# A gated recurrent attention with two MLPs on one core: elementwise steps between VectorE and GpSimd, longer filler pieces, a new order of all steps

## The chip, the core and the metric

The kernel runs on one core of a Trainium2 chip. Of that core's engines it uses TensorE (PE, matrix products), VectorE (DVE), ScalarE (ACT), GpSimd (POOL), and SyncE (SP), whose queue issues all DMAs. The metric is the device time of one execution in microseconds; the lower the better.

## The reference, cut to what matters

A recurrence over 768 steps for 2 x 8 heads of 40, its output as 1536 tokens of 320, then two MLPs over these tokens. All data is float32.

```python
def _attn_ref(q, k, v, i_gate, f_gate, o_gate):      # (2, 8, 768, 40), gates (2, 8, 768)
    for t in range(S):
        m_new = np.maximum(f_gate[:, :, t] + m, i_gate[:, :, t])
        f_stab = np.exp(f_gate[:, :, t] + m - m_new)
        i_stab = np.exp(i_gate[:, :, t] - m_new)
        m = m_new
        C = f_stab[...] * C + i_stab[...] * np.einsum('bhd,bhe->bhde', vt, kt)
        n = f_stab[...] * n + i_stab[...] * kt
        h_tilde = np.einsum('bhde,bhe->bhd', C, qt)
        denom = np.maximum(np.abs(np.einsum('bhd,bhd->bh', n, qt)[:, :, None]), 1.0)
        y[:, :, t] = sigmoid(o_gate[:, :, t]) * h_tilde / denom

def _moe_ref(x, w_a, w_b, w_out):                    # 1536x320, 320x1536 twice, 1536x320
    return (x @ w_a) * (x @ w_b) @ w_out

def _moe2_ref(x, w_in, w_out):                       # 320x2048, 2048x320
    h = x @ w_in
    return (h * sigmoid(h)) @ w_out
```

## The kernel before

The 1536 tokens are twelve tiles of 128 (`u0` to `u11`; even tiles belong to the first batch entry, odd ones to the second). The recurrence is worked out a tile at a time: products of queries and keys (`s0`, "scores"), weighed on DVE with running products of the forget gates (`w0 w1`), times the values (`v0 v1`); what the tile adds to the state (`upd`) and what the state gives to the tile (`car`). Around them stand small steps: scaled keys and values (`sk sv si`), the state carried on (`am`, or `ao ae`, `bo be`), the output's parts put together (`cb0 cb1 cc`), its denominator (`da dn rc`), the gate (`sig om`), the tile of 320 outputs (`ox xt`), its transposes on PE (`px`) and the split of these into a high and a low part (`xh xl`).

The gates of all steps come first, on DVE and ACT: a scan (`run0` for the first 128 steps, `run1` for the other 640), sums and differences (`pl mi ii`), exponentials (`expf expi`), a second scan (`pr`), columns by transposes on PE (`pg0`, copied out by DVE), and the decay factors of the first four tiles by products on PE (`u0.f0` to `u3.f0`) that DVE scans (`d0`).

Float32 products run as float32r products of split operands: every operand is kept as a high part and the rest. For the weights of the first MLP (twelve tiles `w0` to `w11` of 128 hidden columns) this is `p s0 s1 o0 o1` (put together from the loaded words), `h t` (high parts), `u la lb` (the rest; `u` goes by two small DMAs `v0 v1`). For the second MLP's sixteen tiles it is `p s o h ho l t lo` of `x0` to `x15`. `lw` and `lx` load them; `l0.k`, `l0.t`, `l2.e` load queries and keys, the `kvo` tile and stored gate factors.

An MLP pass holds some token tiles and walks over hidden tiles: `m0` two token tiles and hidden tiles 0 to 4, `m1` the next two, `m2` these four with hidden tiles 5 to 11, `m3` and `m4` four tiles each with all twelve; `n0 n1 n2` are the second MLP, four token tiles and sixteen hidden tiles each. For a hidden tile, `a` and `b` are eight PE products each into a PSUM bank (the "h" products; the second MLP has `b` alone), `e` moves a's out, `g` multiplies with b's (for the second MLP `g` is the activation), `h` takes the high part, `l` the rest, `c` is the second layer: three products of 320 columns for each token tile, added up in "acc" banks. `z0` to `z3` evict a pass's token tiles and, in the second MLP, store them.

All of it stands in one hand-written list, ORDER. The program walks over it and issues each step's instructions; an engine runs its own instructions in that order, and waits on semaphores for others. A suffix sets the engine of a step that has a choice: `:v` is DVE, `:p` POOL. Without a suffix, a copy goes to ACT and a two-operand step (`both`, `rest`) to POOL. Eight PSUM banks go round; the hidden tiles have two buffers for each of `g` (by `e` or `g`) and `g2` (by `h` and `l`), two raw buffers take the first MLP's loaded weights.

Thirty steps `f0` to `f29` are fillers: products of a bfloat16 identity with itself into a bank that nobody reads. All of them are placed ahead of the first MLP's products.

Of the kernel before, what the change touches and what calls it, by code (L numbers as in the profile page):

```python
# [68 lines left out]
m3.7.g m3.11.c m4.1.a m3.7.h m3.7.l y1.px y1.xh y1.xl m3.9.h m3.9.l m4.1.b x0.lo lx2 x2.p x2.s x2.o x2.h x2.ho x2.t
m3.7.c m3.9.c m3.z1 m3.z3 m3.z0 y5.xt m4.7.a m4.7.e lx3 x3.p x3.s x3.o x3.ho m3.z2 x2.l x3.lo m4.7.b m4.7.g m4.7.h  # L70
x3.h y2.px y2.xh y2.xl m4.7.l x3.l m4.3.a m4.3.e m4.3.b m4.3.g m4.3.h m4.3.l x2.lo x3.t m4.1.e:v m4.1.g lx5 y3.px
m4.0.a m4.0.e y3.xh m4.0.b m4.0.g m4.10.a m4.3.c m4.10.b m4.7.c m4.2.a m4.1.h:p m4.1.l m4.1.c x5.p x5.s x5.o x5.h
x5.ho x5.l x5.t m4.10.e:v m4.10.g m4.10.h m4.10.l m4.10.c lx10 y3.xl x10.p x10.s x10.o m4.0.h m4.0.l x5.lo m4.2.e
x10.h x10.l x10.t x10.ho x10.lo lx9 x9.p x9.s x9.o x9.h x9.ho x9.lo m4.2.b m4.2.g m4.5.a m4.5.e:v m4.5.b m4.5.g
y0.px y0.xh y0.xl m4.0.c m4.8.b lx4 x4.p m4.11.b m4.11.a x9.l x9.t m4.4.a m4.5.h m4.5.l m4.5.c m4.11.e m4.11.g
m4.11.h m4.11.l m4.4.b lx8 x8.p x8.s x8.o x8.h x8.t x8.ho x8.lo x4.s x4.o x4.ho x8.l x4.lo m4.2.h:p m4.2.l m4.8.a
m4.8.e y4.xt m4.11.c x4.h x4.t x4.l m4.8.g m4.8.h m4.8.l n0.5.b n0.5.g n0.5.h m4.4.e m4.4.g lx13 x13.p x13.s m4.6.b
m4.9.b lx7 x7.p x7.s x13.o x13.ho x13.h x13.l x7.o x7.h x13.t x7.t x13.lo x7.ho x7.lo m4.2.c m4.6.a m4.6.e:v m4.6.g
m4.6.h m4.9.a m4.8.c n0.0.b m4.6.l m4.6.c n0.5.l m4.9.e m4.9.g m4.9.h y7.xt y7.px n0.0.g n0.0.h y5.px y5.xh y5.xl
x7.l n0.7.b lx6 x6.p x6.s x6.o m4.4.h:p m4.4.l m4.4.c y4.px y4.xh m4.9.l m4.9.c m4.z1 m4.z0 y9.xt m4.z2 n0.7.g m4.z3  # L80
n0.0.l lx12 x12.p x12.s x12.o n0.3.b n0.0.c x6.h x6.t n0.5.c n0.8.b n0.7.h n0.7.l x12.ho n0.7.c n0.3.g n0.3.h y7.xh
y7.xl y4.xl n0.3.l n0.9.b n0.8.g n0.8.h x6.ho x6.l n0.6.b n0.6.g n0.8.l n0.8.c x12.h n0.9.g n0.9.h y8.xt n0.9.l
x12.l n0.1.b n0.3.c x12.t y6.xt n0.1.g n0.1.h n0.1.l n0.9.c n0.13.b n0.10.b n0.4.b n0.6.h n0.6.l x6.lo x12.lo lx14
# [24 lines left out]
def tile_mlstm_gated_mlps(ctx: ExitStack, tc: tile.TileContext, i_gate, f_gate, q_cols, k_cols, kvo, w1, w2,  # L108
# [26 lines left out]
    const = ctx.enter_context(tc.tile_pool(name="const", bufs=1))  # L135
# [26 lines left out]
    x1 = {u: const.tile([P, 3 * P], F32, name=f"x1_{u}") for u in range(LAST)}  # L162
# [182 lines left out]
    f0, gs = fg, mm[:, 0:S]  # L345
# [378 lines left out]
    for n in range(FILL):  # L724
        parts[f"f{n}"] = lambda: warm(4)
# [94 lines left out]
```

## Time and profile before

| | |
|---|---|
| median of 3 runs | 441.72 us (439.6 to 442.14) |
| the profiled execution | 440.8 us, of which the span from the first to the last instruction 439.0 us |
| mean granted clock of PE | 0.992 |
| busy | PE 429.1, DVE 151.4, ACT 183.5, POOL 221.5 us |
| DMA | 39.73 MB, 90 GB/s mean |

The span is one profiled execution; the times of the runs include what lies around it. [...] A busy PE need not be a PE at full clock: the same product then takes longer. In the views below, h and acc name the banks of the first and second layer, L245 is a rest or another two-operand step, L412 a filler, L460 the scores, L491 the state update, L611 a first-layer product.

### The profile page before, as it was taken

The page shows a single profiled execution, that of the slowest core. Times are in us where ns is not written, and L with a number is a line of the kernel's source. Part 1 is how long each engine was busy: PE and PEld are TensorE (multiplying, and loading weights), DVE is VectorE, ACT ScalarE, POOL GpSimd, SP SyncE. Part 2 cuts the span into 40 slices and gives each one's busy share as a digit, 9 for nine tenths or more (in the row PEclk, how much of TensorE's full clock was granted, in tenths as well). Part 3 has the DMA queues.
Part 4 walks back from the last instruction along what each step waited for, and adds up shares of the span by engine and source line. Part 5 has one row for each costly group of instructions (what it writes and reads, how often), then busy time and mean ns, then how long its engine had stood idle before and what let it go on. Part 6 is the DMA issues. An engine that isn't in the chain of part 4 may idle for free.

```text
span 439.0 us, 9341 instructions
## 1 busy us (share of the span) xinstructions
PE 429.1 (98%) x3888; PEld 385.6 (88%) x3888; DVE 151.4 (34%) x296; ACT 183.5 (42%) x361; POOL 221.5 (50%) x263
## 2 busy tenths in 40 slices
PE   6799999999999999999999999999999999999996
PEld 6699998898888889888888889989999998989896
DVE  7576776724553544644453333013000100000000
ACT  5657767611211201345342745436343333253243
POOL 4478878657443252354562675355733333235252
PEclk9799999999999999999999999999999999999999
DMA  7869957500604600123230434010010000010001
GB/s 272 266 215 295 274 185 238 173 9 29 193 3 125 220 1 1 47 87 134 66 131 7 134 125 131 2 66 1 0 46 15 1 1 1 0 62 1 1 0 60
DMA packets 16394, 39.73 MB, mean 90 GB/s; under 512 B 2176, under 2 KB 10048, under 8 KB 16352
## 3 DMA queue, kind: packets, MB, share of 16 engines
q1 hardware_dynamic: 16352, 39.14, 27.4%
q8 instruction: 30, 0.49, 0.5%
q14 instruction: 12, 0.10, 0.1%
HBM read 36.34 MB, written 2.01 MB: 87 GB/s over the span
## 4 chain that ended last, share of the span: by engine, by line
PE 94%; DMA 3%; ACT 1%; POOL 0%; issue 0%; SPq 0%; ACTq 0%; POOLq 0%
PE h L611 51%; PE acc L620 11%; PE acc L622 11%; PE acc L621 11%; DMA raw_j<-in_w_dram 3%; PE v_u L473 2%; PE px_u L583 2%; PE s_u L460 2%; PE y_u L480 1%; PE y_u L491 1%; PE warm L412 1%; PE fb_u L428 1%; POOL g2w L245 0%; ACT cvt_j L262 0%; ACT top_j L269 0%
## 5 line engine op out<-in xcount | busy, mean ns | idle before, releaser
L611 PE MATMUL h<-xring,w_j 128*128 128x512 f32 (+1 forms) x1040 | 233.4, 376 | 0.0
L611 PEld LDWEIGHTS h<-xring,w_j 128*128 128x128 f32 x1040 | 181.9, 188 | 31.5
L245 POOL TENSOR_TENSOR g2w<-gw,g2w 128x512 fp32r<-128x512 f32 x48 | 62.7, 1309 | 91.7 <-ACT g2w L240 83.4
L245 POOL TENSOR_TENSOR w_j<-cvt_j,w_j 128x320 fp32r<-128x320 f32 (+3 forms) x72 | 59.6, 836 | 28.3 <-ACT w_j L240 25.5
L245 POOL TENSOR_TENSOR g<-g,g 128x512 fp32r<-128x512 f32 (+1 forms) x41 | 47.9, 1170 | 41.9 <-ACT g L240 41.1
L622 PE MATMUL acc<-w_j,g2w 128*128 128x320 f32 x192 | 59.5, 310 | 0.1
L620 PE MATMUL acc<-w_j,g2w 128*128 128x320 f32 x192 | 59.4, 309 | 0.0
L621 PE MATMUL acc<-w_j,g2w 128*128 128x320 f32 x192 | 59.3, 309 | 0.0
L655 ACT ACTIVATE gw<-h 128x512 f32<-128x512 f32 x48 | 28.4, 597 | 51.0 <-PE h L611 39.2
L620 PE MATMUL acc<-w_j,g 128*128 128x320 f32 x144 | 45.6, 316 | 0.0
L622 PE MATMUL acc<-w_j,g 128*128 128x320 f32 x144 | 44.5, 309 | 0.0
L621 PE MATMUL acc<-w_j,g 128*128 128x320 f32 x144 | 44.5, 309 | 0.0
L240 ACT CAST g2w<-gw 128x512 fp32r<-128x512 f32 x48 | 29.8, 621 | 30.8 <-PE acc L622 30.2
L240 ACT CAST w_j<-cvt_j 128x320 fp32r<-128x320 f32 (+3 forms) x54 | 29.3, 562 | 26.7 <-DVE cvt_j L231 17.3
L652 DVE TENSOR_TENSOR g<-g,h 128x512 f32<-128x512 f32 (+1 forms) x41 | 25.3, 620 | 41.1 <-PE h L611 22.5
L620 PEld LDWEIGHTS acc<-w_j,g2w 128*128 128x128 f32 x192 | 36.1, 188 | 1.2
L621 PEld LDWEIGHTS acc<-w_j,g2w 128*128 128x128 f32 x192 | 36.1, 188 | 1.2
L622 PEld LDWEIGHTS acc<-w_j,g2w 128*128 128x128 f32 x192 | 36.0, 188 | 0.5 <-POOL g2w L245 0.4
L240 ACT CAST g<-g 128x512 fp32r<-128x512 f32 (+1 forms) x30 | 16.8, 561 | 42.7 <-DVE g L652 28.2
L593 DVE TENSOR_TENSOR xring<-px_u,xring 128x384 fp32r<-128x384 f32 x24 | 12.9, 554 | 62.3 <-ACT xring L240 62.0
L620 PEld LDWEIGHTS acc<-w_j,g 128*128 128x128 f32 x144 | 27.1, 188 | 1.1
L621 PEld LDWEIGHTS acc<-w_j,g 128*128 128x128 f32 x144 | 27.1, 188 | 0.7
(92 smaller groups left out, 440.5 us busy)
## 6 DMA issues: line engine op xcount, KB each, us to landing
raw_j<-in_w_dram SPq DMA_DIRECT2D x16, 704.0 KB
raw_j<-in_w_dram SPq DMA_DIRECT2D x11, 960.0 KB
kvo_u<-in_kvo_dram SPq DMA_DIRECT2D x12, 480.0 KB
e_u<-fsd SPq DMA_DIRECT2D x16, 128.0 KB
out_dram<-osb SPq DMA_DIRECT2D x12, 160.0 KB
qk_u<-in_k_cols_dram SPq DMA_DIRECT2D x12, 120.0 KB
qk_u<-in_q_cols_dram SPq DMA_DIRECT2D x12, 120.0 KB
qk_u<-in_k_cols_dram SPq DMA_DIRECT2D x12, 80.0 KB
```

Of the source, the lines that this page charges most:

```text
L240: nc.scalar.copy(out=out_, in_=in_)
L245: (nc.vector if how.get("e") == "v" else nc.gpsimd).tensor_tensor(out=out_, in0=x, in1=y, op=op)
L460: nc.tensor.matmul(out=T["s"][half][t, n], lhsT=x[:, 1, i, t], rhs=x[:, 0, i, t], start=True, stop=True)
L473: nc.tensor.matmul(out=T["V"][t, h], lhsT=un["e", u][t, h], rhs=T["v"][t, h], start=True, stop=True)
L583: nc.tensor.transpose(p[:, i], x[:, i * P:(i + 1) * P], ident)
L593: nc.vector.tensor_tensor(out=xt[:, 3:6], in0=px.pop(u), in1=xt[:, 0:3].bitcast(F32), op=ALU.subtract)
L611: nc.tensor.matmul(out=po, lhsT=w[:, wi:wi + P], rhs=xt[:, :, xi], start=(n == 0), stop=(n == len(pairs) - 1))
L620: nc.tensor.matmul(out=o, lhsT=hi, rhs=w[:, off[0]:off[0] + DM], start=first, stop=False)
L621: nc.tensor.matmul(out=o, lhsT=hi, rhs=w[:, off[1]:off[1] + DM], start=False, stop=False)
L622: nc.tensor.matmul(out=o, lhsT=lo, rhs=w[:, off[0]:off[0] + DM], start=False, stop=last)
L652: nc.vector.tensor_tensor(out=Q[j], in0=Q[j], in1=PB.pop(j), op=ALU.mult)
L655: nc.scalar.activation(out=Q[j], in_=PB.pop(j), func=ACT.Silu, scale=1 / WS)
```

## The change

Steps of two SBUF operands that the program placed on POOL alone can now have the suffix `:v`, and some do; the function `both` already heard it. From POOL to DVE go 23 `l` steps of the first MLP and 14 others (`u` three, `la` one, `lb` two of the weights; `sk sv om ao` two each of the tiles). The high parts `h` of the first MLP go from ACT 30, POOL 11 to ACT 15, POOL 16, DVE 10; five weight copies `w.h` go from ACT to POOL; a few more copies change engines. A filler step has six products where it had four; there are thirty in both. ORDER holds the same 1327 steps in another sequence. No other line differs. The first and last lines of the list, and the filler:

```diff
 ORDER = """
-li const sel f19 f18 f5 f11 f16 f29 f15 f25 lf run0 pl0 ii0 mi0 run1 expi0 expf0 st0 pr0 pl1 mi1:p pg0 u0.f0 u1.f0
-lw0.a w0.pa w0.s0 w0.o0 lw0.b w0.s1 w0.pb w0.o1 w0.h w0.t:p w0.la lw1 w1.s0 ii1 f26 w1.p f7 f23 f8 f27 l0.t u0.sv
-u0.d0 u0.sk l0.k u0.s0 lw2 l1.k u1.d0 w1.s1 w1.o1 w1.o0 f28 u0.si expi1 u0.upd u0.w0 f0 f13 f24 f12 f6 l1.t w0.u
-w0.v1 w0.v0 w0.lb u0.w1 u0.v1 expf1 st1 lw4 pr1 ge w2.s0 w1.h w1.u w1.v1 u0.am u0.car u0.cb0 u0.cb1 u0.v0 f21 f9 f20
-w2.p w2.o0 u0.cc u1.sk u1.s0 u1.w1 w2.s1 w2.o1 u1.si u1.sv u2.f0 u1.w0 u0.sig u0.om u0.da u0.dn u0.rc u0.ox w1.t
-u1.upd u1.v1 u1.am u1.car u1.cb0 u1.cb1 u1.v0 u1.cc w1.lb u0.xt:p u0.px f17 gr w2.h w2.la u2.d0 u3.f0 f10 u1.sig
-u1.om gk u1.da u1.dn u1.rc u1.ox w4.s1 u3.d0 pg1 f4 f3 w2.u u0.bo u0.be w1.la w2.lb u0.xh u0.xl u1.xt u1.px u1.xh
-u1.xl w4.p w4.o1 w4.s0 w2.t w4.o0 w4.h f1 f14 f2 f22 u1.bo u1.be l2.k u2.s0 w1.v0 m0.0.b m0.1.a l2.t u2.sk u2.sv
...
-n2.11.h n2.11.l n2.11.c n2.2.g n2.12.g n2.12.h n2.12.l n2.12.c n2.2.h n2.2.l n2.2.c n2.z0 n2.z1 n2.z2 n2.z3
+li const sel f21 f8 f13 f20 f22 f15 f16 lf f11 f17 f4 run0 run1 pl0 ii0 mi0 ii1 expf0 st0 expi0 pr0 pl1 mi1:p lw0.b
+w0.pb lw0.a w0.pa pg0 l0.t u0.sv w0.s0 u0.si w0.s1 w0.o0 w0.o1 w0.h:p f23 w0.t:p u0.f0 u0.d0 u0.sk lw1 w1.p w1.s0
+w1.o0 w1.s1 w1.o1 expf1 w1.t expi1 w1.h u1.f0 u1.d0 f6 l0.k u0.s0 u0.w0 u0.w1 u0.upd l1.t f5 f14 l1.k lw2 f27 f29
+f28 f1 w0.u w0.v0 w0.v1 u0.v1 st1 u1.sv u1.sk pr1 ge u0.am u0.car u0.cb0 u0.v0 u0.cb1 u0.cc u1.s0 u1.w0 u1.si u1.upd
+f12 f0 w1.u f10 f19 u0.sig u0.om u0.da u0.dn w1.lb u1.w1 u0.rc u0.ox w0.la u1.am u1.car u1.cb0 w1.la u1.cb1 u1.v0
+u1.v1 u1.cc w2.p w2.s0 w2.o0 w2.s1 u1.da u1.dn w2.o1 w2.t:p u1.sig u1.rc u2.f0 u2.d0 f26 f25 u1.om u1.ox gr gk u0.bo
+u0.be w2.h u0.xt w2.lb w2.u lw4 u1.xt w4.p pg1 f24 u3.f0 u3.d0 u0.px u0.xh u0.xl f2 f9 u1.px u1.xh u1.xl f3 f7 f18
+u1.bo w1.v0 l2.k u2.s0 u1.be w4.s1 w4.o1 l2.t u2.sig u2.sk u2.si u2.w1 m0.1.a m0.0.b w4.s0 w4.o0 u2.sv u2.upd u2.ao
+u2.ae lw3 w3.s0 u2.v1 w0.lb w2.la u2.w0 u2.car u2.cb0 w4.h w4.u:v u2.bo u2.be w3.s1 w3.p l3.t u3.sv m0.1.e u3.ao
...
+n2.11.b n2.9.l n2.9.c n2.0.g n2.0.h n2.0.l n2.0.c n2.8.g n2.14.h n2.12.b n2.14.l n2.14.c n2.8.h n2.8.l n2.8.c n2.6.b
+n2.10.g n2.12.g n2.12.h n2.12.l n2.12.c n2.11.g n2.11.h n2.11.l n2.11.c n2.10.h n2.10.l n2.10.c n2.6.g n2.6.h n2.6.l
+n2.6.c n2.z0 n2.z2 n2.z3 n2.z1
 """.split()
...
-        parts[f"f{n}"] = lambda: warm(4)
+        parts[f"f{n}"] = lambda: warm(6)
```

Ahead of the first scores (`u0.s0`) stand 13 filler steps before and 12 after; between these and the first product of `m0`, 17 and 18.

## Rows read from the trace of the kernel before

**Rows 1.** The page, part 1: busy us, share of the span, instructions of each engine.
```profile
PE 429.1 (98%) x3888; PEld 385.6 (88%) x3888; DVE 151.4 (34%) x296; ACT 183.5 (42%) x361; POOL 221.5 (50%) x263
```

**Rows 2.** Windows: start:end, length, busy of PE to POOL, clock, DMA share, GB/s.
```profile
6.00:13.60 7.60, 5.24 (x126) 4.49 (x123) 6.82 (x12) 6.24 (x11) 5.97 (x8) 1.00 0.97 355
13.60:17.00 3.40, 3.40 (x57) 3.03 (x54) 2.28 (x5) 0.00 (x0) 0.92 (x2) 0.50 0.80 269
20.40:23.80 3.40, 3.40 (x71) 3.09 (x70) 2.30 (x6) 2.23 (x5) 2.80 (x4) 0.50 0.84 313
31.70:178.00 146.30, 146.27 (x1918) 131.18 (x1912) 81.91 (x182) 56.21 (x122) 85.90 (x117) 1.00 0.43 133
178.00:430.00 252.00, 252.00 (x1386) 226.51 (x1385) 47.41 (x65) 105.84 (x200) 115.14 (x113) 1.00 0.14 46
```

**Rows 3.** Waits of PE: us in total, times, longest.
```profile
PE warm L412 <- DVE side L704: 2.8, 1, 2.8
PE s_u L460 <- DMA qk_u<-in_q_cols_dram: 2.1, 1, 2.1
PE y_u L480 <- ACT mid_u L240: 1.4, 1, 1.4
```

**Rows 4.** Timeline of PE in the head: start, us, what, count, idle before.
```profile
12.74 0.68 PE L460 MATMUL s_u<-qk_u 40*64 40x64 f32 x28 [0.27 <-issue]
...
13.35 0.41 PE L412 MATMUL warm<-idb 128*128 128x128 bf16 x4
...
14.71 2.32 PE L412 MATMUL warm<-idb 128*128 128x128 bf16 x20
...
24.01 0.60 PE L491 MATMUL y_u<-vx_u,kvo_u 64*64 64x41 f32 x30
...
30.10 1.06 PE L412 MATMUL warm<-idb 128*128 128x128 bf16 x16
...
31.08 0.69 PE L460 MATMUL s_u<-qk_u 40*64 40x64 f32 x32
...
31.71 2.18 PE L611 MATMUL h<-xring,w_j 128*128 128x256 f32 x16
```

**Rows 5.** Timeline of DVE in the head.
```profile
4.32 1.53 DVE L354 TENSOR_TENSOR_SCAN scratch<-scratch 16x640 f32<-16x640 f32 x1
...
7.11 0.17 DVE L391 COPY isg<-pg 128x32 f32<-128x32 f32 x1
...
8.44 0.81 DVE L348 TENSOR_TENSOR scratch<-scratch 16x640 f32<-16x640 f32 x1
...
13.44 0.76 DVE L466 TENSOR_TENSOR e_u<-s_u,e_u 128x256 f32<-128x256 f32 x2 [0.65 <-PE s_u L460]
```

**Rows 6.** Groups by form: busy us, mean ns of one.
```profile
L611 PE MATMUL h<-xring,w_j 128*128 128x512 f32 x880 | 212.5, 392 | 0.0
...
L652 DVE TENSOR_TENSOR g<-g,h 128x512 f32<-128x512 f32 x31 | 21.1, 686 | 40.1 <-PE h L611 22.5 <-ACT g L645 17.3
...
L245 POOL TENSOR_TENSOR g<-g,g 128x512 fp32r<-128x512 f32 x31 | 40.5, 1309 | 39.5 <-ACT g L240 38.9
```

**Rows 7.** Timeline, DVE and POOL: a step alone, and two that meet.
```profile
239.22 0.89 DVE L231 SCALAR_TENSOR_TENSOR cvt_j<-raw_j,cvt_j 128x704 uint32<-128x704 uint32 x1
...
263.10 1.86 DVE L231 SCALAR_TENSOR_TENSOR cvt_j<-raw_j,cvt_j 128x704 uint32<-128x704 uint32 x1
...
264.17 1.94 POOL L245 TENSOR_TENSOR g2w<-gw,g2w 128x512 fp32r<-128x512 f32 x1
```

**Rows 8.** Timeline of the last 9 us: ACT, then POOL.
```profile
430.15 0.62 ACT L240 CAST g2w<-gw 128x512 fp32r<-128x512 f32 x1 [0.66 <-PE acc L622]
...
434.46 1.76 ACT L675 ACTIVATE osb<-acc 128x320 f32<-128x320 f32 x4 [1.99 <-PE acc L622]
...
430.91 1.29 POOL L245 TENSOR_TENSOR g2w<-gw,g2w 128x512 fp32r<-128x512 f32 x1 [2.30 <-ACT g2w L240]
```

**Rows 9.** The chain that ended last: start, us, what; one acc product.
```profile
420.08 0.15 PE acc L622
```

More of the change, by code (lines that the diff above doesn't have):

```diff
@@ L80 @@
[L80 to L83, printed above, removed]
-x14.p x14.s x14.o x14.ho x14.h x14.l x14.lo n0.2.b n0.6.c n0.2.g n0.10.g n0.10.h n0.10.l y6.px y6.xh y6.xl n0.1.c
@@ new lines @@
+m2.5.a u4.rc u4.ox m1.4.e m1.4.g u4.xt u4.px m2.6.e m2.6.g m1.4.h u5.da u5.dn lw9 m2.6.h w9.p w9.s1 w9.s0 u5.rc
+w7.t:p u4.xh u5.ox u5.xt:v w7.v0 w7.la m2.7.a w7.v1 m2.7.b w9.o1 m1.4.l:v w9.t m2.6.l:v w9.o0 w9.h:p w9.u:v w9.lb
+w9.la l6.t w5.v1 m2.5.b m1.4.c u7.si m2.7.e m2.7.g m2.7.h:p lw10 w10.s0 w10.s1 m1.z0 w8.la:v w8.v0 m2.8.a m1.z1
+w10.p w10.o1 w10.o0 m2.7.l:v w10.h:p w10.u w10.lb w10.la u5.px u5.xh u4.xl m2.5.e m2.5.g lw11 w11.p w9.v1 m2.9.b
+w11.s0 w11.o0 w9.v0 m2.9.a m2.9.e:v m2.9.g m2.7.c m2.6.c l7.e w10.t w11.s1 m2.9.h:v w11.o1 w11.h w8.v1 w11.t m2.8.b
@@ new lines @@
+l8.t u8.sig u8.sv l9.e u9.d0 m2.11.b m2.11.e m2.11.g m3.2.a m3.2.b m2.11.h:p m3.2.e:v m3.1.a l8.e u8.d0 u8.sk
+m2.11.l:v m2.11.c m3.2.g m2.z1 y1.xt u8.ao:v m2.z3 l9.k l9.t u9.sk m2.z0 m2.z2 m3.1.b m3.1.e m3.1.g u8.upd u8.ae
+u9.s0 u9.w0 u9.w1 l8.k u8.s0 u8.w0 u8.car u8.cb0 m3.2.h m3.2.l u9.sv u9.si u9.v0 u9.upd u9.v1 u8.v0 u9.ao u9.ae
+u9.car u8.w1 u8.v1 u8.cb1 u8.cc u8.bo u8.be u8.om u8.da u8.dn u8.rc u8.ox u8.xt m3.3.a m3.3.e:v m3.3.b m3.3.g
+m3.3.h:v m3.3.l u9.cb1 u9.cb0 u10.si:v u9.cc u9.da u9.sig u9.dn u9.rc u9.om:v u9.ox u9.xt:v m3.5.a m3.2.c m3.3.c
@@ new lines @@
+m4.2.g lx4 x4.p x4.s x4.o x4.ho m4.2.h:p m4.2.l:v x4.h x4.t x4.l x9.lo y4.xt m4.11.a m4.5.b m4.5.a m4.6.b m4.10.c
+lx13 x4.lo m4.5.e:v m4.5.g m4.5.h n0.5.b n0.5.g m4.9.a m4.5.l m4.5.c m4.9.b lx8 x8.p x8.s x8.o x8.h x8.t x8.ho x8.lo
+m4.6.g m4.9.e:v m4.9.g x13.p x13.s x13.o x13.ho x13.lo m4.6.h:p m4.6.l:v x13.h x13.t n0.2.b m4.2.c x13.l x8.l
+m4.11.e:v lx6 x6.p x6.s x6.o x6.ho m4.11.b m4.11.g m4.11.h:v m4.11.l:v n0.0.b n0.0.g m4.4.a n0.0.h n0.0.l m4.4.e
+m4.6.c m4.9.h:p m4.9.l:v m4.4.b m4.4.g m4.11.c lx7 n0.2.g x7.p x7.s x7.o x7.ho x7.lo x7.h x7.l x6.lo m4.4.h:p
@@ new lines @@
+m4.4.l:v x7.t m4.8.a m4.8.e m4.8.b n0.3.b y4.px m4.9.c y5.xt y5.px m4.8.g m4.8.h:p y5.xh y5.xl y6.px y6.xh y6.xl
+m4.4.c x6.h n0.5.h y4.xh y4.xl m4.8.l m4.8.c m4.z1 y9.xt m4.z0 y8.xt x6.l m4.z3 n0.0.c n0.5.l n0.5.c x6.t n0.6.b
+n0.7.b n0.3.g lx11 y11.xt x11.p n0.3.h n0.3.l m4.z2 n0.2.h n0.3.c lx12 x12.p x12.s x12.o x12.h x12.l x12.ho x12.lo
+n0.7.g n0.7.h x12.t n0.9.b n0.8.b y7.px y7.xh y7.xl n0.2.l n0.2.c n0.8.g n0.1.b n0.7.l n0.7.c n0.10.b n0.8.h n0.8.l
+n0.8.c x11.s n0.6.g x11.o x11.ho x11.lo n0.6.h n0.6.l x11.h x11.t x11.l n0.11.b n0.6.c n0.10.g lx14 n0.9.g x14.p
@@ new lines @@
+n0.9.h lx15 x15.p n0.9.l n0.9.c n0.4.b n0.10.h n0.10.l n0.10.c x14.s x15.s x15.o x15.ho n0.1.g n0.1.h x15.lo n0.1.l
+n0.1.c n0.4.g n0.4.h n0.12.b n0.4.l n0.4.c x14.o x14.ho x14.lo y8.px x15.h x15.t x15.l x14.h x14.t x14.l n0.12.g
+n0.12.h n0.12.l n0.14.b n0.12.c n0.15.b n0.11.g n0.11.h n0.11.l y10.xt n0.14.g n0.14.h n0.11.c n0.15.g n0.15.h
+y10.px n0.13.b y10.xh y10.xl y11.px y11.xh y8.xh n0.14.l y8.xl y11.xl n0.15.l n0.15.c n0.14.c n0.13.g n0.13.h
+n0.13.l n1.2.b n1.2.g n1.2.h n0.13.c n0.z1 n1.6.b n0.z3 n1.6.g n1.5.b n0.z2 n1.2.l n1.2.c n1.4.b n1.6.h n1.6.l
@@ new lines @@
+n1.6.c n1.5.g n1.5.h n1.5.l n1.5.c n0.z0 n1.9.b n1.9.g n1.13.b y9.px n1.4.g n1.4.h n1.0.b n1.1.b n1.4.l n1.4.c
+n1.9.h n1.9.l n1.9.c n1.1.g n1.1.h n1.8.b n1.1.l n1.1.c n1.0.g n1.0.h n1.0.l n1.0.c y9.xh y9.xl n1.13.g n1.13.h
+n1.13.l n1.10.b n1.10.g n1.10.h n1.10.l n1.13.c n1.15.b n1.3.b n1.3.g n1.10.c n1.12.b n1.7.b n1.3.h n1.15.g n1.15.h
+n1.15.l n1.15.c n1.3.l n1.3.c n1.8.g n1.8.h n1.8.l n1.14.b n2.13.b n1.12.g n1.12.h n1.12.l n1.12.c n2.13.g n1.11.b
+n1.8.c n1.7.g n1.7.h n1.7.l n1.7.c n1.14.g n1.14.h n2.15.b n1.14.l n1.14.c n1.11.g n1.11.h n1.11.l n1.11.c n1.z0
```

96 lines of the change are left out of this document (35 added, 61 removed).

## The prediction

> **What bounds the kernel now.** I began with the page's busy times: TensorE (PE below) is busy 429.1 of 439.0 us, the next engine half of that [rows 1]. So the question was where PE is not at work, and I took the windows table, cut at the places where the granted clock changes [rows 2]. [...] What the kernel loses lies in the head. The waits of PE, the next view, have three entries of weight: 2.8 us at the very start, before the identity is there, 2.1 us on the landing of the q and k columns, 1.4 us on a copy by ScalarE (ACT) [rows 3]. [...]
>
> **The fillers.** Both kernels play thirty filler pieces; the products go from 120 to 180. A filler product costs what the timeline shows: sixteen take from 30.10 to 31.08, 0.061 us each, at full clock, twenty take 2.32 us, 0.116 each, at half [rows 4]. Sixty more are 3.7 us at full clock, 7.0 at half, all before the first h product. Whether they are paid depends on what they stand in for, so I sort them by place. Ahead of the first scores the new order has 12 pieces (72 products) where the old has 13 of four (52). In the old kernel the scores wait 2.1 us for their columns, and most of them run from 12.74 to 13.35 [rows 3, 4]. The new order moves one 480 KB load of `kvo` ahead of a weight load, but both stay ahead of these columns, so the bytes in front of them are the same and I leave the landing where it is. The 20 extra products, 1.2 to 2.3 us, fall into that wait and are free. Behind the scores the old order has 68 products to the first h product, the new one 18 pieces, 108 products: 40 more, 2.4 us at full clock, on PE's path.
>
> **The head as a sum.** From the end of the first scores, 13.35, to the first h product, 31.71 [rows 4], is 18.36 us. Out of it come the wait of 1.4 us for ACT's copy [rows 3] and the two losses of 1.7 us [rows 2]: 13.6 us of work at full clock. The pieces of work up to the first h product are the same in both orders (scores, updates, carries and values of tiles 0 and 1, decay factors of four tiles, transposes of two, scores of tile 2), so the new head needs 13.6 + 2.4 = 16.0 us behind 13.35, if nothing waits: first h product at 29.35 with no stretch at half clock, 31.05 with one, 32.75 with two.
>
> **Does something wait in it?** The gate chain comes first. The long scan `run1` (1.53 us) now stands ahead of `pl0 ii0 mi0` on VectorE (DVE), so the first gate columns, copied at 7.11 before, come up to 1.5 us later; I take 1.2, since `run1` no longer stands between that chain and `st0` [rows 5]. From that copy to the end of the weighing at 14.20 DVE took 7.1 us with 0.65 idle; the same instructions without `ii1` (0.8 us, now done before) from 8.3 on end at 14.0, and at 15.4 if the second weight tile is 1.4 us later for the `kvo` load (480 KB at 355 GB/s [rows 2]). PE comes to the value products at 13.35 + 0.6 (thirty update products [rows 4]) + 36 x 0.061 = 16.1. So DVE is in time by 0.7 us at least: the fillers cover it, and without them the wait would be there. ACT's copy `u0.am` no longer stands behind the third weight tile's conversion, which waited for a DMA; the new order puts `w2.p` behind `u1.am`. I take the 1.4 us as gone. On SyncE's queue (SP) the loads of tile 1 (`l1.t l1.k`) now go out ahead of `lw2`, whose issue has to wait for a raw buffer; they were queued behind that wait before. `lw2` loses at most the two loads' bytes, about 0.9 MB or 2.5 us at the same rate, and `w2` is first used at the third h block, some 4 us behind the first. At the head's end, PE's own work between tile 1's last value product and its transposes grows from 3.4 to 5.2 us, and from these to the first h product it stays (1.5, 1.6), so the x columns are not later for PE than before.
>
> **The clock.** The wait for the columns shrinks from 2.1 us to about 1.1, and 0.3 remains inside the scores. Before, 1.4 us of waiting was enough to bring a stretch at half clock [rows 2, 3]; 1.1 + 0.3 is as much, in two parts. So one stretch is likeliest; none and two are rivals.
>
> **Operations moved to DVE.** 37 steps on two SBUF operands go from POOL to DVE, 23 of them the `l` steps of the first MLP: 1.31 us each on POOL, 0.69 us for the nearest DVE row, which has one operand in PSUM [rows 6]. So a chain of `e g h l` gets 0.6 us shorter, and POOL loses some 30 us of work. For PE this is worth nothing, as PE does not wait there, and DVE, busy 82 us of 146 in the stretch up to 178 us [rows 2], has room. The price may be above 0.69: where a two-operand DVE step and a POOL step met, the DVE step took 1.86 us against 0.89 alone, the POOL step 1.94 against 1.29 [rows 7, 8]. That is 0.65 to 0.97 us a meeting. [...] What covers it: eight h products are 8 x 0.24 us, a `c` of four tiles 12 x 0.15 [rows 6, 9]; counted with these over the order, the least PE work between a hidden tile's last h product and its `c` is 3.6 us in the new first MLP (five places under 4 us), and four steps of 0.6 to 0.7 with three hops of 0.14 (the gap from ACT's end to POOL's start at 430.8 [rows 8]) need 3.1, with another 0.3 before `l` is read. So a meeting of 0.97 may just stick out, by 0.2.
>
> **The tail.** The order of the last evictions becomes 0, 2, 3, 1. They ran back to back, 0.44 us each, as the tiles were finished [rows 8]; now the second waits its turn to the end: +0.44 us. The last four `c` instead of three stand behind the last h block, each with a 1.29 us `l` behind an ACT copy that needs the buffer of the `c` before last. The old tail let PE idle for some tenths on this (the last `l` but one runs from 430.91 to 432.20, ahead of its `c`); I give the new one the same, within 0.5 either way.
>
> **Sum.** The profiled execution took 440.8 us, 439.0 of it span. One half-clock stretch: 31.05 - 31.71 + 0.44 = -0.2: **440.6 us**. The runs' median of 441.72 is 0.9 above the profiled execution and their lowest 1.2 below; stretches at half clock, 1.7 us each, are of that size, and I put no offset on the forecast.
>
> **Rivals.** [...] (2) *Two stretches*: 32.75 - 31.71 + 0.44 = +1.5: 442.3; the 40 products behind the scores are then pure cost. It needs a second wait in the head; the sum above finds none. (3) *The middle starts to wait*, slower than before: two-operand steps on DVE and POOL hold each other up, and a `c` comes before its `l`. It decides where meetings add more than the 0.8 us of cover (3.6 + 0.3 - 3.1) at the five tight places. At 0.2 each it is 1 us; with a second meeting in the same chain, 1.1 us each, 5.7: 441.6 to 446.3, and over that if a wait passes the 1.4 us behind which the clock fell. For it: meetings are seen. Against: POOL has less to do, and the old order had places just as tight without a wait. (4) *The change does not reach PE at all* beyond the fillers: the ACT wait stays: 442.0.
>
> **Chances.** One stretch 0.42, none 0.25, two or (4) 0.15, the middle 0.18. A range that leaves out 2 in 10: below, case (1) less the 1.2 us by which runs fall under the profiled one, 437.7; above, case (2) with the 1.3 us by which the highest run stands over it, 443.6, drawn to 444.0 for the nearer half of (3). A change within 1%, 4.4 us, is no change that this kernel's runs tell apart: faster by more needs under 437.3, which only (1) with luck reaches, 0.05; slower by more needs (3) at its upper end, 0.07; within, 0.88.
>
> **What would show it.** In the profile after: the first h product between 29.3 and 31.1; PE's waits in the head under 1.5 us behind the first filler; one stretch at 0.50 or none; no PE wait from there to 430; the `l` steps on DVE at 0.7 us, 1.3 and more where they meet POOL; the last eviction 0.4 us later behind the last product. I am wrong if PE waits in the middle, if the columns land later than before because three loads now crowd behind them, or if the clock falls twice.

## The result and the profile after

The changed kernel takes 443.38 us (median of 20 runs, 439.88 to 448.05), the kernel before on the same chip 440.13 us (20 runs, 437.92 to 442.52): ratio 1.0067, 95% interval 1.0041 to 1.0094. It is 0.7% slower, where the forecast was no change (-0.2 us). The profiled execution took 442.93 us, 441.2 of it span. Ratios here leave out runs over 1.5% above their kernel's fastest; medians and means are over all runs (by means 443.79 against 440.13).

I read the same views as before, in the same order. Line numbers are those of each run's own file, up to three off the kernel before's; PEld is TensorE's weight loads. The page's busy times come first, with a row that the first reading had skipped, a queue that carries instructions:

```profile
PE 430.9 (98%) x3948; PEld 387.8 (88%) x3948; DVE 175.2 (40%) x347; ACT 171.5 (39%) x341; POOL 192.1 (44%) x232
...
q8 instruction: 31, 0.51, 0.5%
```

Against [rows 1] PE has the 60 filler products more and is busy 1.8 us longer; POOL lost 29 us, DVE gained 24. The moves happened as the diff says. The second row says that 31 pieces of instructions, 0.51 MB or 16 KB each, came by DMA during the run. By the count they are PE's: its 7896 products and weight loads make 255 for each of the 31, the kernel before's 7776 make 259 for each of its 30 (0.49 MB), and the sixteen profiles of this document have 30 or 31 such pieces, each one for every 256 of PE's instructions.

The windows, cut where PE's behaviour changes (the columns are those of [rows 2]):

```profile
6.00:14.70 8.70, 7.37 (x184) 6.71 (x181) 6.59 (x12) 7.61 (x15) 5.07 (x8) 1.00 0.96 330
14.70:30.90 16.20, 14.99 (x410) 13.84 (x407) 12.42 (x30) 10.48 (x24) 10.92 (x17) 1.00 0.83 276
...
13.57:30.94 17.37, 16.16 (x464) 14.92 (x455) 13.59 (x31) 11.51 (x26) 11.71 (x19) 1.00 0.84 278
...
123.50:129.80 6.30, 5.28 (x258) 5.11 (x258) 3.27 (x10) 0.00 (x0) 2.08 (x4) 1.00 0.03 11
129.80:133.20 3.40, 3.40 (x9) 2.61 (x9) 1.49 (x6) 0.43 (x2) 0.80 (x1) 0.50 0.37 93
...
178.00:430.00 252.00, 252.00 (x1382) 226.19 (x1381) 57.43 (x87) 101.34 (x193) 103.03 (x104) 1.00 0.14 46
```

The head has no stretch at half clock any more, where [rows 2] had two. But 1.2 us of 16.2 are idle in it, and in the middle, where [rows 2] had 0.03 us idle in 146, PE now stands for 1.0 us between 123.5 and 129.8, while ACT did nothing, DVE was idle half the time and POOL two thirds of it, and directly behind that comes a stretch at 0.50: 3.4 us, of which half, 1.7 us, is lost.

PE's waits (answering to [rows 3]):

```profile
PE warm L414 <- DVE side L706: 2.8, 1, 2.8
PE y_u L493 <- issue: 1.3, 2, 1.0
PE s_u L462 <- DMA qk_u<-in_q_cols_dram: 0.9, 1, 0.9
PE fb_u L430 <- issue: 0.9, 1, 0.9
PE s_u L462 <- DVE cvt_j L275: 0.4, 1, 0.4
```

The wait for ACT's copy is gone. New at this size (the kernel before had one of 0.3 us) are waits ended by "issue": the profile shows no engine and no data that released PE. The timeline shows how odd they are, in the head and at 126 us:

```profile
12.42 0.33 PE L462 MATMUL s_u<-qk_u 40*64 40x64 f32 x4 [0.93 <-DMA qk_u<-in_q_cols_dram]
13.16 0.62 PE L462 MATMUL s_u<-qk_u 40*64 40x64 f32 x26 [0.41 <-DVE cvt_j L275]
13.57 0.20 PE L493 MATMUL y_u<-vx_u,kvo_u 64*64 64x41 f32 x2
...
22.26 0.85 PE L430 MATMUL fb_u<-scratch,ident 128*64 128x64 f32 x21
24.01 0.56 PE L430 MATMUL fb_u<-scratch,ident 128*64 128x64 f32 x11 [0.89 <-issue]
...
30.94 1.33 PE L613 MATMUL h<-xring,w_j 128*128 128x256 f32 x9
...
125.90 0.51 PE L493 MATMUL y_u<-vx_u,kvo_u 64*40 64x41 f32 x17
127.43 0.32 PE L493 MATMUL y_u<-vx_u,kvo_u 64*40 64x41 f32 x9 [1.02 <-issue]
```

PE stops in the middle of a group: 21 products of one kind run, then nothing for 0.9 us, then 11 more with the same operands. A wait for these operands can't look like that, since the first product of the group had them.

Where the 2.2 us of span went (441.2 against 439.0): the first h product comes 0.8 us earlier (30.94, [rows 4] 31.71); from it to the start of PE's last product it is 406.25 us against 403.73, 2.5 us more, the stand and the half-clock stretch; and the end comes 3.96 us behind that start, not 3.59.

### The profile page after: what moved, and what is told of

The parts are those of the page before. It is cut to its first block, busy times and chain, and to the rows that moved or that the text cites. A ratio compares the mean times of both kernels' runs of the same rounds, so it can differ in the third digit from the quotient of the medians.

```text
span 441.2 us, 9483 instructions
## 1 busy us (share of the span) xinstructions
PE 430.9 (98%) x3948; PEld 387.8 (88%) x3948; DVE 175.2 (40%) x347; ACT 171.5 (39%) x341; POOL 192.1 (44%) x232
## 4 chain that ended last, share of the span: by engine, by line
PE 95%; DMA 2%; ACT 1%; issue 1%; SPq 0%; POOL 0%; DVE 0%; ACTq 0%; DVEq 0%; POOLq 0%
PE h L613 51%; PE acc L622 11%; PE acc L624 11%; PE acc L623 11%; PE v_u L475 2%; PE px_u L585 2%; DMA raw_j<-in_w_dram 2%; PE s_u L462 2%; PE y_u L493 2%; PE warm L414 1%; PE y_u L482 1%; PE fb_u L430 1%; POOL g2w L247 0%; ACT cvt_j L264 0%; SPq L208 0%
## 5 line engine op out<-in xcount | busy, mean ns | idle before, releaser
L247 POOL TENSOR_TENSOR g2w<-gw,g2w 128x512 fp32r<-128x512 f32 x48 | 61.8, 1293 | 97.5 <-ACT g2w L242 92.5
L247 POOL TENSOR_TENSOR w_j<-cvt_j,w_j 128x320 fp32r<-128x320 f32 (+3 forms) x69 | 57.5, 844 | 39.9 <-ACT w_j L242 38.1
L242 ACT CAST w_j<-cvt_j 128x320 fp32r<-128x320 f32 (+3 forms) x47 | 23.6, 528 | 31.6 <-DVE cvt_j L233 24.8
L654 DVE TENSOR_TENSOR g<-g,h 128x512 f32<-128x512 f32 (+1 forms) x41 | 25.3, 618 | 23.6 <-PE h L613 17.9
L247 POOL TENSOR_TENSOR g<-g,g 128x512 fp32r<-128x512 f32 (+1 forms) x18 | 19.8, 1101 | 23.4 <-DVE g L244 16.5
L622 PEld LDWEIGHTS acc<-w_j,g 128*128 128x128 f32 x144 | 27.0, 188 | 1.1
L623 PEld LDWEIGHTS acc<-w_j,g 128*128 128x128 f32 x144 | 27.1, 188 | 0.8
L624 PEld LDWEIGHTS acc<-w_j,g 128*128 128x128 f32 x144 | 27.0, 188 | 0.0
```

The costliest lines, as they stand in the source:

```text
L242: nc.scalar.copy(out=out_, in_=in_)
L247: (nc.vector if how.get("e") == "v" else nc.gpsimd).tensor_tensor(out=out_, in0=x, in1=y, op=op)
L622: nc.tensor.matmul(out=o, lhsT=hi, rhs=w[:, off[0]:off[0] + DM], start=first, stop=False)
L623: nc.tensor.matmul(out=o, lhsT=hi, rhs=w[:, off[1]:off[1] + DM], start=False, stop=False)
L624: nc.tensor.matmul(out=o, lhsT=lo, rhs=w[:, off[0]:off[0] + DM], start=False, stop=last)
L654: nc.vector.tensor_tensor(out=Q[j], in0=Q[j], in1=PB.pop(j), op=ALU.mult)
```

## The theories

**A.** PE's instructions arrive in pieces of 256 (the 31 of 16 KB above; a product and its weight load are two). A assumes that the fetch of the next piece begins when PE crosses into one, and that PE, if it is through before the next has come, stands. The new order makes two runs of 128 small products into one of 256 (tiles 8 and 9; before, `m3.3.a` stood between them). In this execution PE crossed into a piece at 124.0, the packet of the next one ran from 124.9 to 125.8, PE was through at 126.4 and went on at 127.43. So the piece lasted PE 2.4 us and the next one took 3.4 us from the crossing (0.9 to the packet, 0.9 for it, 1.6 until PE went on), which leaves the 1.0 us of the stand. The half clock behind it is the second part of the price.

**B.** The longer fillers cost more in the head than they save.

**C.** VectorE steps that meet GpSimd's make the middle wait (the third rival).

## Experiments

"Lost" is what the half clock took: span times (1 - mean granted clock, the share of full clock in a run's record), averaged over the runs of a kernel. "Left" is the mean time without it. A "plus or minus" below is a 95% interval from the scatter of the runs. A stand is a stretch in which PE does nothing. Each group has the kernel before beside it on the same chip; the changed kernel ran beside e13 and e14 alone, so that differences from its 443.38 (mean 443.79) in 1 to 9 are across measurements, and the kernel before's own medians differ by 0.9 us between them.

| kernel | median us | ratio (95%) | lost us | left us |
|---|---|---|---|---|
| e1_split_run | 441.53 | 1.0028 (0.9997-1.0059) | 0.66 | 440.83 |
| e2_whole_run_in_before | 441.34 | 1.0037 (1.0009-1.0065) | 2.57 | 438.71 |
| e3_fill4 | 441.72 | 1.0036 (1.0003-1.0069) | 3.76 | 438.67 |
| e4_rest_on_pool | 450.11 | 1.022 (1.0182-1.0259) | 2.54 | 446.98 |
| before, beside e1 to e4 | 439.67 | | 3.12 | 436.96 |
| e5_wide_fill | 444.28 | 1.0088 (1.0057-1.0119) | 3.41 | 441.45 |
| e6_split_wide_z | 441.94 | 1.0045 (1.0021-1.007) | 1.76 | 440.51 |
| e7_before_wide_fill | 439.65 | 1.0007 (0.9973-1.0042) | 3.56 | 437.47 |
| e8_before_fill6 | 440.65 | 1.002 (0.9989-1.0051) | 0.81 | 440.24 |
| before, beside e5 to e8 | 439.90 | | 3.36 | 437.22 |
| e9_before_moves | 447.17 | 1.014 (1.0087-1.0193) | 2.61 | 445.31 |
| e10_split_fill4_z | 439.85 | 0.9959 (0.992-0.9999) | 2.65 | 438.13 |
| e11_shift | 441.72 | 1.004 (1.0003-1.0077) | 1.15 | 441.20 |
| e12_load_later | 441.23 | 1.0018 (0.998-1.0055) | 3.28 | 438.58 |
| before, beside e9 to e12 | 440.61 | | 3.32 | 437.07 |
| e13_change_again | 443.64 | 1.0061 (1.0032-1.0091) | 2.70 | 441.01 |
| e14_split_z | 440.83 | 1.0005 (0.9972-1.0039) | 0.81 | 440.34 |
| before, beside e13, e14 | 440.58 | | 2.92 | 437.82 |

**1. The run split again (in the changed kernel).**

```diff
-... u9.sv u9.si u9.v0 ... u8.ox u8.xt m3.3.a m3.3.e:v m3.3.b
+... u9.sv u9.si m3.3.a m3.3.e:v u9.v0 ... u8.ox u8.xt m3.3.b
```

> The changed kernel with the eight first-layer products of m3.3.a (and their eviction) moved from behind the small products of tiles 8 and 9 into their middle, where the kernel before has them. Theory A (code): TensorE's instructions come by DMA in pieces of 16 KB, enough for about 128 products; the unbroken run of 256 small products at 123.5 us uses them up faster than they come, TensorE stands about 1.0 us on issue, and the clock then falls for 3.4 us, 1.7 us of work: 2.7 us together. Then here the issue wait near 126 us is under 0.3 us, there is no half-clock stretch at 130 us, and the time falls by 1.5 to 2.7 us, to a ratio of 1.000 to 1.004 to the kernel before. Theory B (the 60 more filler products are the loss, 2.4 to 3.7 us) and theory C (two-operand steps on VectorE and GpSimd hold each other up until TensorE waits): nothing changes, ratio 1.0067 within 0.002.

The windows of e1 over that stretch, and its waits:

```profile
120.00:134.00 14.00, 14.00 (x299) 12.14 (x298) 8.55 (x21) 1.54 (x5) 4.97 (x7) 1.00 0.13 45
...
PE y_u L490 <- issue: 2.7, 1, 2.7
```

PE is busy in all 14 us, at full clock. The median fell by 1.85 us (the mean by 2.3, plus or minus 1.3), and the time lost at the half clock from 2.73 (mean of the changed kernel's 20 runs) to 0.66. The second row is a stand in the head, at 18.4 us, at a place where the list of instructions is the changed kernel's own: the head's stands differ from execution to execution, 1.2 us there, 2.7 here.

**2. The long run in the old order.**

```diff
-... m3.1.l m3.3.a m3.3.e u9.si:p ... u8.v0 u8.v1 u8.cb0
+... m3.1.l u9.si:p ... u8.v0 u8.v1 m3.3.a m3.3.e u8.cb0
```

> The kernel before with one edit: m3.3.a and its eviction moved behind the last value product of tile 8, so that the two runs of 128 small products at 124 and 128 us become one of 256. Nothing of the change is in it. Theory A: an issue wait of about 1 us in the second half of the run, a half-clock stretch behind it in some executions, 1 to 2.7 us slower, ratio 1.002 to 1.006. Theories B and C: no wait, ratio 1.000 within 0.002.

It was slower as A expects, but not by A's mechanism. PE stands 0.9 us at 126, and the timeline of e2 shows POOL, then PE:

```profile
125.61 1.27 POOL L243 TENSOR_TENSOR g<-g,g 128x512 fp32r<-128x512 f32 x1 [1.20 <-ACT g L238]
126.83 0.19 POOL L240 COPY vx_u<-isg 128x8 f32<-128x8 f32 x1
...
127.07 0.60 PE L489 MATMUL y_u<-vx_u,kvo_u 64*64 64x41 f32 x30 [0.89 <-POOL vx_u L240]
...
43.67 0.31 PE L619 MATMUL acc<-w_j,g 128*128 128x320 f32 x1
45.66 0.41 PE L620 MATMUL acc<-w_j,g 128*128 128x320 f32 x1 [1.68 <-issue]
```

A small copy that PE needs stood behind an `l` step of 1.27 us on POOL's queue: a wait for data, brought about by my edit. The pieces lay otherwise in this order (crossed at 125.6, the next reached at 131.3), so this run says nothing of A at that place. It does at another: at 43.67 PE stops between two products of one accumulation, the packet that it waited for ran from 43.1 to 44.3, and behind this stand of 1.7 us the clock did not fall.

**3. Fillers of four, and fillers made wide, in the changed kernel.**

```diff
-        parts[f"f{n}"] = lambda: warm(6)
+        parts[f"f{n}"] = lambda: warm(4)
```

> The changed kernel with filler pieces of four products as before (120 products, not 180). Theory B: the 40 products behind the scores were on TensorE's path: 2.4 us at full clock come back, ratio 1.000 to 1.002. Theory A: the run near 126 us and its issue wait are unchanged; in the head the code of 60 products less has to come, but TensorE arrives earlier at steps that were covered by fillers and waits there, and the clock may fall: between 1 us faster and 1.5 us slower than the changed kernel, ratio 1.004 to 1.010. Theory C: as A.

```diff
-        for _ in range(n):
-            nc.tensor.matmul(out=un["warm"], lhsT=idb, rhs=idb, start=True, stop=True)
+        for _ in range(n // 3):
+            nc.tensor.matmul(out=un["warm"], lhsT=idb, rhs=idb.unsqueeze(1).to_broadcast([P, 3, P]), start=True, stop=True)
```

> The changed kernel with each filler piece made of two products of 384 columns in place of six of 128: the same columns and so the same time on TensorE, a third of the instructions (60 products in place of 180). The order stays. Theory A (code: TensorE stands because its instructions come too slowly): the issue waits of the head (0.3 and 0.9 us in the profile of the changed kernel) go, the one near 126 us stays; 0.5 to 1.5 us faster than the changed kernel, ratio to the kernel before 1.003 to 1.006. Theory B (the fillers' time on TensorE is what costs): nothing changes, ratio 1.0067 within 0.002, first h product not before 30.5 us.

e3's median is 1.7 us under the changed kernel's, e5's 0.9 over it; by means both are within the noise (1.4 less and 1.1 more, each plus or minus 1.8 or more). A's gain for e5 (0.5 to 1.5 us) was missed: fewer instructions did not mean less waiting. With fewer filler instructions the crossings in the head come earlier, among the loads: in e5 PE crossed at 12.7, the packet began only at 17.6, and PE stood 2.9 us from 17.3. But these two runs hold the plainest evidence on A. Both took products away ahead of the run of 256 (60 and 120), so pieces begin elsewhere in it. The timelines, e3 and then e5:

```profile
128.50 0.19 PE L482 MATMUL y_u<-cn_u,qk_u 40*64 40x41 f32 x1 [0.79 <-issue]
```

```profile
130.24 0.44 PE L493 MATMUL y_u<-vx_u,kvo_u 64*40 64x41 f32 x18 [1.37 <-issue]
```

Counting PE's records in order of start: in the changed kernel 166 products of the run stand ahead of the stop, in e3 225, in e5 158. From the start of the program these are products 1986, 1985 and 1858: the same count twice, to within one product, and one piece (128 products) less. The stop is tied to the count of instructions and not to a product, its data or the moment. The count holds nearly everywhere: the sixteen profiles have 28 waits of PE of 0.5 us or more that "issue" ended, and 24 of them stand where exactly 193 + 256 n of PE's instructions have started (449, 705, 961, 1473, 1729, 2241, 3777, 4033). The other four come before 13 us, three in front of PE's 41st product and one in front of the first scores. In all 24 PE went on 1.25 to 1.61 us after the end of a packet of the instruction queue.

The time that a piece lasts sorts the cases behind 90 us. Six times in the sixteen profiles PE was through a piece in under 3 us: in the changed kernel, e13, e3, e4 and e5 (2.4 to 2.8 us) a stand of 0.8 to 1.4 us followed; the sixth is e11 (part 9), whose packet came early. Behind pieces of 4 us and more no such stand followed there.

**4. The moved steps back on GpSimd, in the new order.**

```diff
-        (nc.vector if how.get("e") == "v" else nc.gpsimd).tensor_tensor(out=out_, in0=x, in1=y, op=op)
+        nc.gpsimd.tensor_tensor(out=out_, in0=x, in1=y, op=op)
```

> The changed kernel, its order and fillers, with every step of two SBUF operands back on GpSimd (the 37 steps moved to VectorE). Theory C: the loss goes, ratio 1.000 to 1.002. Theories A and B: TensorE's run near 126 us is unchanged and so is the loss, ratio 1.006 or more (up to 2 us more where an l step on GpSimd now takes 1.3 us ahead of its c).

```profile
PE acc L624 <- POOL g L247: 2.7, 1, 2.7
...
PE h L613 <- POOL w_j L247: 1.3, 1, 1.3
```

By medians it is 6.7 us slower than the changed kernel, and PE now waits for POOL. The stand in the run of 256 is there again (0.95 us, at the same instruction 4033). C falls: in the new order the steps on DVE carry no wait of PE, and without them it has some.

**5. Only the moves, in the old order.** 37 steps get `:v`; order and fillers stay.

```diff
-... m0.2.l w3.h ... m0.1.l ...
+... m0.2.l:v w3.h ... m0.1.l:v ...
```

> The kernel before in its own order and with its own fillers; only 37 of the operations that the change put on VectorE stand there too. A (TensorE stands where its next piece of 256 instructions isn't there yet): the moves don't touch TensorE's list, so no such stand is added; ratio to the kernel before 0.998 to 1.002, granted clock as before. C (slow VectorE operations beside GpSimd's make the middle wait): TensorE waits on the moved operations, ratio 1.003 to 1.01. Pieces crossed and fetched as in the kernel before.

A expected nothing, C up to 1%; it is 1.4% slower. The timeline of e9 at PE's longest such wait, DVE, POOL, PE:

```profile
266.63 0.53 DVE L226 TENSOR_SCALAR cvt_j<-cvt_j 128x704 uint32<-128x704 uint32 x1 [0.19 <-ACT cvt_j L221]
267.19 0.89 DVE L230 SCALAR_TENSOR_TENSOR cvt_j<-raw_j,cvt_j 128x704 uint32<-128x704 uint32 x1
268.00 1.29 DVE L244 TENSOR_TENSOR g<-g,g 128x512 fp32r<-128x512 f32 x2
...
265.31 1.30 POOL L244 TENSOR_TENSOR g2w<-gw,g2w 128x512 fp32r<-128x512 f32 x1
...
268.74 0.42 PE L621 MATMUL acc<-w_j,g 128*128 128x320 f32 x1 [1.27 <-DVE g L244]
```

No DVE and POOL steps meet here. The moved `l` steps take 0.65 us each, but they stand behind two weight steps on DVE's queue (0.53 and 0.89), and POOL, which did them in the kernel before, is idle from 266.6 on. A step moved to a faster engine came late, because of what that queue had ahead of it. So the loss is larger than C's, and at its longest wait it is a queue and not a meeting. The waits of the other microseconds (PE is idle 5.5 us between 31 and 430) were not taken apart; one of them, 1.0 us at 38.8, is a stand at instruction 1473, which A had excluded.

**6. Fillers alone, in the old order.** e8: `warm(4)` becomes `warm(6)` in the kernel before. e7: one product of 512 columns in place of four of 128.

> The kernel before with filler pieces of six products in place of four, its order unchanged: this one part of the change alone. Theory B: 40 to 60 products of 0.061 us on TensorE's path, 1.5 to 3.5 us slower unless they fall into the waits, ratio 1.003 to 1.008; theory A: the same columns, and issue waits in the head on top, so the ratio is the same or up to 0.003 higher, and the profile shows issue waits of 0.5 us or more in the head which the kernel before has not.

> The kernel before with each filler piece made of one product of 512 columns in place of four of 128: the same columns, 30 instructions in place of 120. Theory A: the code of 90 products less has to come in the head; its TensorE waits there for a DMA and a copy anyway, so 0 to 1 us faster, ratio 0.998 to 1.000. Theory B: no change, 1.000 within 0.002.

e8 is the cleanest reading of B: lost 0.81 us and not 3.36, left 440.24 and not 437.22. Sixty more products cost 3.0 us and save 2.55 at the half clock: net +0.5, within the interval of nothing. The 3.0 is not products alone: e8's profile has a stand of 1.6 us at instruction 961 (25.3 us), where the profile of the kernel before has none of 0.5 us or more. e7 shows that the form of the filler is worth nothing there.

**7. Split, wide fillers, evictions in the order 0, 1, 2, 3.**

> The changed kernel with three edits: m3.3.a and its eviction in the middle of the run of small products of tiles 8 and 9, filler pieces of two products of 384 columns, and the last evictions in the order 0, 1, 2, 3. Theory A: no issue wait over 0.5 us in the head or near 126 us, the last eviction ends 0.4 us earlier behind the last product; 2.5 to 4 us faster than the changed kernel, ratio 0.997 to 1.001. Theory B: the fillers still cost their 2.4 us, ratio 1.001 to 1.004.

```profile
436.89 1.75 ACT L674 ACTIVATE osb<-acc 128x320 f32<-128x320 f32 x4 [1.95 <-PE acc L621]
```

That row is ACT's tail in e6; the changed kernel's is this:

```profile
436.23 0.44 ACT L677 ACTIVATE osb<-acc 128x320 f32<-128x320 f32 x1 [1.95 <-PE acc L624]
437.10 1.21 ACT L677 ACTIVATE osb<-acc 128x320 f32<-128x320 f32 x3 [0.44 <-PE acc L624]
```

In the changed kernel ACT idles 0.44 us after the first eviction, since the next in its list belongs to a tile not yet finished. The end comes 3.58 us behind the start of PE's last product in e6, 3.96 there: 0.38 us for the order of four evictions. Wide fillers go with stands in the head again (3.1 us). A's number was missed: by medians e6 is 1.4 us under the changed kernel and not 2.5 to 4.

**8. Three edits together, and one load later.** e10: the split, fillers of four, evictions 0 to 3. e12: e10 with `lw2` moved behind `u1.car`.

> The changed kernel with three edits: m3.3.a between the two runs of small products, fillers of four products, the last evictions in the order 0, 1, 2, 3. A: the stand at 126 us and the half-clock stretch behind it go (about 2.5 us), the evictions give 0.38 us, the fillers 0.4 to 1 us in the head; against 443.4 that is 440 to 441, ratio to the kernel before 0.998 to 1.002 where the head has one half-clock stretch, 0.994 where it has none. B (the fillers' length is what the change loses): ratio 1.000 to 1.003, with the stand at 126 still there. Neither expects a stand between 100 and 180 us under A, one of 1 us under B.

> The kernel of the run before last (m3.3.a split off, fillers of four, evictions 0 to 3), and the load of w1's third group of columns (960 KB) is issued some 4 us later, behind the carried products of tile 1. A: the piece that TensorE fetches in that stretch no longer queues behind that load: from crossing to fetch 1 to 1.5 us and not 2.5 to 3, so the stands at pieces in the head (15 to 25 us) sum to under 0.6 us; first h product 0.5 to 1 us earlier than in the kernel with the load in its place, unless the w1 columns then come too late (a DMA wait in front of an h product). If code doesn't queue behind data, the stands stay as they are, 0.6 to 1.3 us.

e10's ratio is 0.9959, at the edge of its interval, but by means over its twelve runs it is at 440.78 against 440.39 for the kernel before: that it is faster than the kernel before is not shown. It is 3.5 us under the changed kernel by medians, 3.0 by means (no stand between 65 and 430 in its profile). e12 settles nothing: the piece crossed at 16.3 was fetched after 0.8 us and not 3.2, as A says, but the next, crossed at 19.8, waited 3.7 behind other loads; in time it is 1.4 us behind e10 by medians, within the noise.

**9. The pieces shifted the other way.** In tile 6 each product of `values` is made twice, the second over the first.

```diff
-                    nc.tensor.matmul(out=T["V"][t, h], lhsT=un["e", u][t, h], rhs=T["v"][t, h], start=True, stop=True)
+                    for _ in range(2 if u == 6 else 1):
+                        nc.tensor.matmul(out=T["V"][t, h], lhsT=un["e", u][t, h], rhs=T["v"][t, h], start=True, stop=True)
```

> The changed kernel, in which each of the 32 products e by v of tile 6 (near 107 us) is made twice, the second time over the first: 32 products (64 instructions with their weight loads) more ahead of the run at 123.5. A: the stand stays at the same count of instructions, 4033, so it comes 32 products earlier in the run: among the products v of tiles 8 or 9 or at the end of tile 8's carried ones, and not behind the 17th update product of tile 9; length 0.5 to 1.3 us. A wait for data or for an engine would stay behind the same update product, at 126.4 plus 0.65 = 127.0 us. Time 443 to 445, ratio 1.006 to 1.012.

The windows of e11, the run of 256 and what follows:

```profile
122.00:129.60 7.60, 7.60 (x269) 6.81 (x268) 5.25 (x15) 1.26 (x4) 3.11 (x5) 1.00 0.07 27
129.60:134.00 4.40, 4.40 (x22) 3.61 (x21) 2.85 (x8) 0.24 (x1) 0.65 (x2) 1.00 0.43 133
```

My expectation missed: the stand didn't move, it went. PE crossed into the piece at 123.9, but this time the next one's packet had begun at 121.8, before the crossing, just ahead of the eight h products (2.0 us) that stand before the run. In this profile the whole run of 256, still there, neither stops PE nor lowers the clock. With 32 products more, 0.65 us of work, the kernel is not slower than the changed one: the median is 1.7 us lower, the mean 1.4, plus or minus 1.7.

What decides when the fetch starts I can say only in part. Between 95 and 135 us, with few loads under way (DMA share 0.26 in the changed kernel, 0.83 in its head), the packets of all profiles began between 3.2 us ahead of the crossing and 1.6 us behind it, with loads queued up to 6.0 us behind. Behind 200 us, at long products alone, all began ahead, by up to 4.6 us, when PE had 1 to 42 instructions of its piece to go (34 in e11 at 121.8). Forty instructions are some 0.4 us of small products (2.4 us for 256) and nearly 5 us of h products (0.24 us for two); by this estimate it helps where long products stand directly ahead of a crossing. That this lead is why e11's stand went is likely, but no other run tests it.

**10. Control.** The changed kernel again, and with the split and the evictions, but its own fillers of six, on one chip.

> The changed kernel, unaltered, as the control beside the next one. A: the stand at 126 us in front of the 167th small product of the run (product 1986 of TensorE's list) and a half-clock stretch behind it in most executions; lost to the half clock (span times one minus the mean granted clock) 2.2 to 3 us on average; ratio 1.004 to 1.010.

> The changed kernel with its fillers of six, m3.3.a between the two runs of small products and the last evictions in the order 0, 1, 2, 3. A (what the change loses is the stand, the half clock behind it and the evictions; the fillers of six cost the head about what they save at the half clock): 2.3 to 3.3 us under the changed kernel, lost to the half clock under 1.2 us on average, ratio to the kernel before 0.999 to 1.003. B (the fillers are what it loses): still 1.004 or more, with little half clock.

The control repeats the result (1.0061), the stand again at product 1986 (1.05 us; in that execution the clock did not fall behind it). e14 is 2.56 us faster by means, 1.89 of it at the half clock (2.70 to 0.81) and 0.67 in the time that is left. It is level with the kernel before. So of the 2.97 us between control and before (443.71 and 440.74), 2.56 (plus or minus 1.5) are the joined run and the evictions, and 0.41 (plus or minus 1.2) is the rest: order, moves and fillers, the last worth 0.5 in e8.

## Why the prediction failed

443.38 lies inside the forecast's range, but that is luck: its upper end came from two half-clock stretches in the head and the scatter of the runs (443.6), drawn on to 444.0 for the third rival, and this head had no such stretch.

**The head.** The sum was right in its parts (its two losses of 1.7 us are half of the two stretches of 3.4 us at 0.50 in [rows 2]). The products behind the first scores start at 13.57, 0.2 later than I set (13.35), behind a wait on DVE. From there to the first h product PE is busy 16.16 us, where I had 16.0, and idle 1.2, two stands of 0.3 and 0.9 us; so the first h product came at 30.94 and not at 29.35. The step that failed is "if nothing waits in it", and with it "the sum above finds none". I asked of each engine and each queue whether it was in time, and not of PE's own instructions. The wait for ACT went, as forecast.

**Fillers and clock.** 2.4 us forecast on PE's path; sixty products cost 3.0 in e8, stands included. I set one half-clock stretch as likeliest; fillers of six leave 0.8 us lost on average (e8, e14) where the kernel before, with fillers of four, loses 2.9 to 3.4, so a head without a stretch (29.35 - 31.71 + 0.44 = -1.9, 438.9, the case (1) of the range and of the chance of 0.25) was nearer. What the longer fillers cost they save there. By that alone the change would have come to about nothing (e14, 1.0005), as the forecast said.

**"No PE wait from there to 430".** This is the step that cost the result. The third rival had the place right, a middle that starts to wait and a clock that falls behind it, and the mechanism wrong: what was short was PE's next piece of instructions in a run of 256 products at 0.02 us each (258 in the 5.28 busy us of the window from 123.5), a term that the sum left at nothing and that measured 1.0 us of stand and, in that profile, 1.7 us at the half clock. [rows 2] shows an unbroken middle, and nothing in it warned of this; the warning was in the order, where a block of h products was taken out between two such runs, and in the instruction queue's row of the page.

Most pieces came in time: 24 stands of 0.5 us or more fall on some 490 crossings (sixteen profiles, 30 or 31 each). In the run of small products the next one came too late: 256 instructions were issued in 2.4 us and it took 3.4, which cost 1.0 us at 127.43; among the loads of the head a stand came to 2.9 us in e5.

**The moves.** "For PE this is worth nothing" holds for the change as a whole: `l` takes 0.735 us on DVE, 0.69 forecast from [rows 6], and PE's waits name none of them:

```profile
L247 DVE TENSOR_TENSOR g<-g,g 128x512 fp32r<-128x512 f32 x20 | 14.7, 735 | 13.6 <-POOL g L244 9.3 <-ACT g L242 4.2
```

But it does not hold of the part: the moves alone cost 6.6 us (e9), order and fillers without the moves 10.4 (e4), and all three with the run split and the evictions in order about nothing (e14). I priced both as if they were independent.

**The tail.** +0.44 forecast from [rows 8], 0.37 to 0.38 measured (3.59 us from the start of PE's last product to the end before, 3.96 after, 3.58 in e6); the cause was right.

**Not settled.** Why the clock falls behind some stands and not behind others (1.7 us in e2 without a fall, 1.0 us in the changed kernel with one in one profile and without in the other); which part of the head's stands the changed order brings, as they vary by 2.4 us between executions with the same list there (0.3 in e13, 2.7 in e1); and what exactly starts a fetch.

## What to carry to other kernels

Where TensorE runs through one or two hundred products of a few tens of columns without a pause, count its instructions: here each 256 were a transfer of their own; the one behind the crossing at 124.0 was there after 3.4 us, 128 small products lasted 2.4, and long products between such runs were the time in which it arrived. Read an idle gap ended by "issue" by its count in the engine's list before looking for a late engine. And an order and a placement that were changed together have to be priced together: each half alone can be far worse than either whole.

## What the runs showed of the hardware

PE's instructions come by DMA while data do (31 packets of 16 KB for the 7896 products and weight loads): in the head, where the DMA share is 0.83, a 16 KB packet began up to 4.9 us after the crossing, against 1.6 at most between 95 and 135 us. That it queues behind the data is the likely reason, but no run isolates it (e12 settled nothing). A packet took 0.9 to 1.8 us, and where PE stood for it, it went on 1.25 to 1.61 us after its end. And adding work need not add time: with 32 products more, 0.65 us of PE's work, a stand of 1.0 us was gone (e11), most likely since they moved where a piece begins.
